# Taking a chunk's decay from a row of exp(-cum) by a small DMA instead of from N=1 products

**Chip, cores, metric.** One core of one Trainium2 chip. The metric is the device time of one execution in microseconds (us). Ratios are the mean time of one kernel's fast runs over that of the other's fast runs of the same rounds, so not quite the ratio of the medians that are quoted beside them.

## The reference

A gated linear recurrence per head, then a dense layer pair with a maximum. Cut to what matters:

```python
f = 1.0 / (1.0 + np.exp(-f_logit))                    # batch 4, heads 8, seq 768, head_dim 48
for t in range(S):
    state = f[:, :, t, :, None] * state + np.einsum('bhd,bhe->bhde', k[:, :, t], v[:, :, t])
    y[:, :, t] = np.einsum('bhd,bhde->bhe', q[:, :, t], state)
# x = y with the heads side by side: 3072 tokens x 384
g = np.maximum(x @ w1, x @ w2)                        # 384 x 1024 each
out = g @ w_out                                       # 1024 x 384
```

## The kernel before

The sequence is cut into 6 chunks of 128 tokens; with 4 batches that makes 24 tiles. For each tile `ell` = ln(1+exp(-f_logit)), and `cum` is its running sum over the tokens, a product with a triangular matrix. From it come `ei` = exp(cum) for k and `ed` = exp(-cum) for q. The state that goes on to the next chunk is multiplied by the decay of the whole chunk, `fl` = exp(-sum of ell over the 128 tokens). `fl` is wanted with the head's 48 features on partitions, while `cum` has tokens there. So the kernel sums again, with four products of one column:

```python
def p_cum(i):
    ps = psum["cum", i] = ps_s.tile([C, 512], F32, name="cum", tag="s")
    nc.tensor.matmul(out=ps[:, 0:dm], lhsT=ut, rhs=ell[:, :, 0:D], start=True, stop=True)
    for p in range(NP if i // B < nch - 1 else 0):              # NP = 4 pairs of heads
        nc.tensor.matmul(out=ps[:, dm + p:dm + p + 1],
                         lhsT=ell[:, 2 * p:2 * p + 2, :].rearrange("p h d -> p (h d)"),
                         rhs=ones_col, start=True, stop=True)
def a_ed(i):                                                    # ScalarE
    t = st[i]["ed"] = work.tile([C, dm], F32, name="ed", tag="ed")
    nc.scalar.activation(t, psum["cum", i][:, 0:dm], AF.Exp, scale=-1.0)
def a_fl(i):                                                    # ScalarE, 128x4
    t = st[i]["fl"] = work.tile([C, NP], F32, name="fl", tag="fl", bufs=5)
    nc.scalar.activation(t, psum["cum", i][:, dm:dm + NP], AF.Exp, scale=-1.0)
def m_qp(i, eng):                                               # GpSimd; k's product is on VectorE
    eng.tensor_mul(s["qp"][:, :, 0:D], ld[i]["q"], s["ed"].rearrange("p (h d) -> p h d", h=H))
def m_st(i):                                                    # GpSimd
    ...   # new state = tmp * fl, broadcast over the other 48 features
```

Every load and every store is issued by SyncE (`nc.sync.dma_start`), five transfers of 192 KB per tile: f_logit, v, q, k and the result. The order of all operations is written out by hand; one tile's step in the middle is

```
st -4  d0 -1  cum 1  a 0  ed 1  d1 -1  g0 -1  am 0  lv 2  qp 1  fl 1  ei 1  lq 3  g1 -1
o0 -1  kpv 1  y 0  tmp -2  lk 3  o1 -1  x 0  e 2  xT 0  tr 1  ln 2  out -4  xTe 0  sa -1
tre 1  ob -1  lf 4  v 1
```

The last steps have a table of their own (the closing steps below).

Of the kernel before, what the change touches and what calls it, by code (L numbers as in the profile page):

```python
# [10 lines left out]
F32 = mybir.dt.float32  # L11
BF16 = mybir.dt.bfloat16
AF = mybir.ActivationFunctionType
# [19 lines left out]
lq 7  o1 3  x 4  st 2  xT 4  lq 9  e 6  tr 5  xTe 4  st 1  sa 3  ln 6  d0 4  tre 5  lf 8  # L33
ob 3  cum 6  g0 4  a 5  v 5  d1 4  ed 6  am 5  lq 8  ei 6  qp 6  g1 4  o0 4  tmp 3  fl 6
out 2  e 7  y 5  kpv 6  o1 4  x 5  lk 8  ln 7  xT 5  tr 6  xTe 5  sa 4  lf 9  d0 5  tre 6
ob 4  cum 7  g0 5  a 6  out 0  v 6  d1 5  ed 7  am 6  ei 7  lv 8  qp 7  g1 5  o0 5  tmp 4
y 6  kpv 7  out 1  o1 5  x 6  st 3  fl 7  xT 6  tr 7  lk 9  e 8  xTe 6  sa 5  ln 8  tre 7
lk 10  ob 5  v 7  lf 10
"""

STEP = """
st -4  d0 -1  cum 1  a 0  ed 1  d1 -1  g0 -1  am 0  lv 2  qp 1  fl 1  ei 1  lq 3  g1 -1
o0 -1  kpv 1  y 0  tmp -2  lk 3  o1 -1  x 0  e 2  xT 0  tr 1  ln 2  out -4  xTe 0  sa -1
tre 1  ob -1  lf 4  v 1
"""
FIRST_STEP = 7
EPILOGUE = """
st 15  d0 18  cum 20  a 19  ed 20  d1 18  g0 18  am 19  qp 20  ei 20  lv 21  g1 18  o0 18
tmp 17  st 16  out 15  y 19  kpv 20  o1 18  x 19  lk 22  e 21  xT 19  tr 20  ln 21  xTe 19
# [14 lines left out]
def kernel(  # L64
# [13 lines left out]
    nc = tc.nc  # L78
    B, H, S, D = q.shape
    C = 128  # L80
    nch = S // C
    dm = H * D
# [3 lines left out]
    DP = 64  # L86
    NP = H // 2
# [3 lines left out]
    consts = ctx.enter_context(tc.tile_pool(name="consts", bufs=1))  # L91
    loads = ctx.enter_context(tc.tile_pool(name="loads", bufs=9))
    work = ctx.enter_context(tc.tile_pool(name="work", bufs=2))
# [8 lines left out]
    qp_b = [consts.tile([C, H, DP], BF16, name=f"qp{n}") for n in range(NQ)]  # L102
    kp_b = [consts.tile([C, H, DP], BF16, name=f"kp{n}") for n in range(NQ)]
    ell_b = [consts.tile([C, H, DP], BF16, name=f"ell{n}") for n in range(2)]
    st_b = [[consts.tile([C, NP, 2 * D], BF16, name=f"st{b}_{n}") for n in range(2)] for b in range(B)]
    ut = consts.tile([C, C], BF16)
    ident = consts.tile([C, C], BF16)
    ones_col = consts.tile([C, 1], BF16)
# [10 lines left out]
    def setup(n):  # L119
        if n == 0:  # L120
            for t in ell_b:
                nc.vector.memset(t, 0.0)
            nc.vector.memset(ones_col, 1.0)
            make_upper_triangular(nc, ut, 1.0, diag=True)
            make_identity(nc, ident)
            for t in (kp_b[0], qp_b[0]):
                nc.vector.memset(t, 0.0)
        elif n == 1:
            nc.vector.tensor_copy(mask, ut.unsqueeze(1).to_broadcast([C, H, C]))
            for t in kp_b[1:] + qp_b[1:]:  # L130
                nc.vector.memset(t, 0.0)
        else:
            for b in range(B):
                for t in st_b[b]:
                    nc.gpsimd.memset(t, 0.0)


    ld = {}
    st = {}
# [37 lines left out]
    psum = {}  # L177
# [33 lines left out]
    def p_cum(i):  # L211
        ell = st[i]["ell"]
        ps = psum["cum", i] = ps_s.tile([C, 512], F32, name="cum", tag="s")
        nc.tensor.matmul(out=ps[:, 0:dm], lhsT=ut, rhs=ell[:, :, 0:D], start=True, stop=True)  # L214
        for p in range(NP if i // B < nch - 1 else 0):
            nc.tensor.matmul(out=ps[:, dm + p:dm + p + 1],  # L216
                             lhsT=ell[:, 2 * p:2 * p + 2, :].rearrange("p h d -> p (h d)"),
                             rhs=ones_col, start=True, stop=True)
# [3 lines left out]
        nc.scalar.activation(t, psum["cum", i][:, 0:dm], AF.Exp)  # L222

    def a_ed(i):
        t = st[i]["ed"] = work.tile([C, dm], F32, name="ed", tag="ed")
        nc.scalar.activation(t, psum["cum", i][:, 0:dm], AF.Exp, scale=-1.0)  # L226

    def a_fl(i):
        if i // B == nch - 1:
            return  # L230
        t = st[i]["fl"] = work.tile([C, NP], F32, name="fl", tag="fl", bufs=5)
        nc.scalar.activation(t, psum["cum", i][:, dm:dm + NP], AF.Exp, scale=-1.0)

    def m_kp(i, eng):
        s = st[i]
# [3 lines left out]
    def m_qp(i, eng):  # L239
        s = st[i]  # L240
        s["qp"] = qp_b[i % NQ]
        eng.tensor_mul(s["qp"][:, :, 0:D], ld[i]["q"], s["ed"].rearrange("p (h d) -> p h d", h=H))  # L242

    def p_tr(i, sel):
        ps = psum["tr" + sel, i] = ps_s.tile([C, len(sel), NP, C], BF16, name="tr", tag="s")
# [45 lines left out]
    def m_st(i):  # L291
        c, b = divmod(i, B)
        if c < nch - 1:
            for o in range(2):
                r, e = slice(o * DP, (o + 1) * DP), slice(o * D, (o + 1) * D)
                nc.gpsimd.tensor_mul(st_b[b][(c + 1) % 2][r, :, e], st[i]["tmp"][r, :, e],  # L296
                                     st[i]["fl"][r, :].unsqueeze(2).to_broadcast([DP, NP, D]))

    def p_y(i):
        c, b = divmod(i, B)  # L300
# [36 lines left out]
    def a_g(i, half):  # L337
        s = st[i]
        if half == 0:
            s["g"] = work.tile([C, FG, C], BF16, name="gT", tag="gT", bufs=3)  # L340
        nc.scalar.activation(s["g"][:, half * 4:half * 4 + 4, :], psum.pop(("d", half, i)), AF.Relu)  # L341

    def p_o(i, half):
        s = st[i]
        if half == 0:
            psum["o", i] = ps_m.tile([C, dm], F32, name="o", tag="mm")
        mms = [(s["xT"][:, j, :], w2o[:, j, :]) for j in range(JG)]
        mms += [(lambda f=f: s["g"][:, f, :], wo[:, f, :]) for f in range(FG)]
        cut = 6
        for n in (range(0, cut) if half == 0 else range(cut, len(mms))):  # L350
            l, r = mms[n]
            nc.tensor.matmul(out=psum["o", i], lhsT=l() if callable(l) else l, rhs=r,  # L352
                             start=(n == 0), stop=(n == len(mms) - 1))
# [22 lines left out]
    def ob_last(h):  # L376
        t = st[T - 1]["ob", h] = consts.tile([C, dm // 2], F32, name=f"obl{h}")
        if h == 0:
            nc.scalar.copy(t, psum.pop(("last", h)))
        else:  # L380
            nc.vector.tensor_copy(t, psum.pop(("last", h)))
# [5 lines left out]
    def warm(n):  # L387
# [5 lines left out]

    ops = {
        "setup": setup, "lf": lambda i: load(i, "f"), "lk": lambda i: load(i, "k"),
        "lq": lambda i: load(i, "q"), "lv": lambda i: load(i, "v"),
        "lw1": lambda n: load_w(w1_f, moe_w1, n), "lw2": lambda n: load_w(w2_f, moe_w2, n), "lwo": load_wo,
        "w2c": cast_w2, "w2ca": lambda j: cast_w2(j, True), "woc": cast_wo,
        "wd": sub_wd, "wdp": lambda j: sub_wd(j, nc.gpsimd),
        "w2T": tr_w2, "w2Te": ev_w2T, "w2o": mm_w2o, "w2oe": ev_w2o,  # L400
        "e": a_e, "ln": a_ln, "v": v_v, "cum": p_cum, "ei": a_ei, "ed": a_ed, "fl": a_fl,
        "kp": lambda i: m_kp(i, nc.gpsimd), "kpv": lambda i: m_kp(i, nc.vector),
        "qp": lambda i: m_qp(i, nc.gpsimd), "qpv": lambda i: m_qp(i, nc.vector),
        "tr": lambda i: p_tr(i, "kq"), "trk": lambda i: p_tr(i, "k"), "trq": lambda i: p_tr(i, "q"),
        "tre": lambda i: v_tr(i, "kq"), "trke": lambda i: v_tr(i, "k"), "trqe": lambda i: v_tr(i, "q"),
        "a": p_a, "am": v_am, "sa": p_sa, "tmp": v_tmp, "st": m_st,
        "y": p_y, "x": a_x, "xT": p_xT, "xTe": v_xT,
        "d0": lambda i: p_d(i, 0), "d1": lambda i: p_d(i, 1),
        "g0": lambda i: a_g(i, 0), "g1": lambda i: a_g(i, 1),
        "o0": lambda i: p_o(i, 0), "o1": lambda i: p_o(i, 1), "ob": v_ob, "out": store, "warm": warm,  # L410
        "lo": p_last, "lob0": lambda n: ob_last(0), "lob1": lambda n: ob_last(1),
        "lout": store_last,
    }
# [4 lines left out]
    def run(op, n):  # L418
        key = (same.get(op, op), n)
        if op == "warm" or key not in done:  # L420
            done.add(key)
            ops[op](n)

    def pairs(text):
        words = text.split()
        return [(op, int(n)) for op, n in zip(words[0::2], words[1::2])]

    for op, n in pairs(PROLOGUE):
        run(op, n)
    last = pairs(EPILOGUE)  # L430
    kept = split_up | {(same.get(op, op), n) for op, n in last}
    for i in range(FIRST_STEP, T + 8):
        for op, n in pairs(STEP):
# [34 lines left out]
```

## Time and profile before

| | before |
|---|---|
| time, median (range) | 146.11 us (146.02 to 146.57), 3 runs |
| span of the profiled run | 144.2 us |
| period of a tile, with and without the N=1 products | 4.97 and 4.90 us |
| issues on SyncE's DMA queue per tile | 5 |
| spacing of f_logit's last 12 loads ("load pace" below) | 4.86 us |

Three more groups of the page are needed to compare (columns: line, engine, operation, output and input, count, then busy us and mean ns of one, then idle time before it and its releaser):

```profile
L242 POOL TENSOR_TENSOR qp<-qt,ed 128x384 bf16<-128x384 f32 x22 | 22.3, 1013 | 61.7 <-ACT ed L226 31.6
L226 ACT ACTIVATE ed<-cum 128x384 f32<-128x384 f32 x24 | 11.8, 493 | 16.5 <-PE cum L216 13.1
L237 DVE TENSOR_TENSOR kp<-kt,ei 128x384 bf16<-128x384 f32 x23 | 14.1, 613 | 0.5 <-ACT ei L222 0.5
```

And the timeline of SyncE's DMA queue over one tile (start us, duration us of the issue):

```profile
75.58 1.59 SPq L148 DMA_DIRECT2D ft<-in_f_logit_dram  x1
77.23 0.57 SPq L148 DMA_DIRECT2D vt<-in_v_dram  x1
77.89 0.77 SPq L148 DMA_DIRECT2D qt<-in_q_dram  x1
78.71 1.13 SPq L148 DMA_DIRECT2D kt<-in_k_dram  x1
79.93 0.87 SPq L362 DMA_DIRECT2D out_dram<-ob  x1
```

Each of these issues begins some 0.05 to 0.1 us after the one before has ended.

### The profile page before, as it was taken

What the parts mean: (1) busy time and instruction counts of PE and PEld (TensorE: products, weight loads), DVE (VectorE), ACT (ScalarE), POOL (GpSimd) and SP (SyncE); (2) the same over time, 40 slices, a digit from 0 to 9 for tenths busy, and PEclk for the clock granted to TensorE, in tenths of its full rate; (3) what the DMA queues carried; (4) which work ended last, traced back from release to release, by engine and by line L of the source; (5) the groups of instructions that cost most, each with busy time, mean ns of one, the idle gap of its engine ahead of it and who ended that gap; (6) DMA issues with size and microseconds to landing.
All of it is one profiled execution on the core that took longest, in us unless ns stands there. A gap on an engine that the chain in (4) does not pass through costs nothing.

```text
span 144.2 us, 4442 instructions
## 1 busy us (share of the span) xinstructions
PE 130.0 (90%) x1820; PEld 101.3 (70%) x1820; DVE 104.4 (72%) x191; ACT 88.6 (61%) x199; POOL 54.6 (38%) x80
## 2 busy tenths in 40 slices
PE   0197499999899999999999999999999999999981
PEld 0044366677678877887887788778878877777771
DVE  7234988766989778877977797798779777976520
ACT  3572548877387566658566765766585667663440
POOL 8320060230556066236524632652364246362000
PEclk9999999999999999999999999999999999999999
DMA  4999999999999999999898999989899998971111
GB/s 93 271 362 386 341 303 154 188 188 140 206 174 196 188 213 221 173 227 233 166 203 183 215 208 210 219 181 196 182 198 222 190 251 180 225 223 57 59 55 55
DMA packets 104612, 28.60 MB, mean 198 GB/s; under 512 B 100368, under 2 KB 103568, under 8 KB 104592
## 3 DMA queue, kind: packets, MB, share of 16 engines
q1 hardware_dynamic: 104592, 28.32, 90.1%
q8 instruction: 14, 0.23, 0.7%
q14 instruction: 6, 0.05, 0.1%
HBM read 23.59 MB, written 4.72 MB: 196 GB/s over the span
## 4 chain that ended last, share of the span: by engine, by line
PE 72%; SPq 19%; DMA 4%; DVE 1%; issue 1%; ACT 0%
PE o L352 25%; PE d L334 22%; SPq L148 13%; PE tr L249 6%; PE a L267 5%; SPq L153 5%; DMA vt<-in_v_dram 4%; PE y L312 3%; PE y L307 2%; PE xtp L322 2%; PE cum L214 2%; PE sa L281 2%; SPq L157 1%; PE o L373 1%; DVE am L272 1%
## 5 line engine op out<-in xcount | busy, mean ns | idle before, releaser
L242 POOL TENSOR_TENSOR qp<-qt,ed 128x384 bf16<-128x384 f32 x22 | 22.3, 1013 | 61.7 <-ACT ed L226 31.6
L334 PE MATMUL d<-xT,wd 128*128 128x128 bf16 x576 | 40.6, 220 | 0.8 <-DVE xT L326 0.4
L352 PE MATMUL o<-wo,gT 128*128 128x384 bf16 x184 | 37.4, 325 | 0.0
L334 PEld LDWEIGHTS <-wd 128*128 128x128 bf16 x576 | 34.4, 114 | 3.8 <-DVE wd L175 0.6
L341 ACT ACTIVATE gT<-d 128x512 bf16<-128x512 f32 x48 | 29.0, 604 | 10.1 <-PE d L334 10.0
L272 DVE TENSOR_TENSOR am<-a,mask 128x1024 bf16<-128x1024 f32 x24 | 29.4, 1224 | 0.7 <-PE a L267 0.7
L296 POOL TENSOR_TENSOR st<-tmp,fl 64x192 bf16<-64x192 f32 x40 | 25.5, 638 | 1.6
L326 DVE COPY xT<-xtp 128x384 bf16<-128x384 bf16 x24 | 8.6, 358 | 21.1 <-PE xtp L322 21.1
L352 PEld LDWEIGHTS <-gT 128*128 128x128 bf16 x184 | 16.1, 97 | 9.1 <-ACT gT L341 0.2
L226 ACT ACTIVATE ed<-cum 128x384 f32<-128x384 f32 x24 | 11.8, 493 | 16.5 <-PE cum L216 13.1
L258 DVE COPY trs<-tr 128x1024 bf16<-128x1024 bf16 (+1 forms) x27 | 17.0, 631 | 2.9 <-PE tr L249 1.1
L317 ACT CAST x<-y 128x384 bf16<-128x384 f32 x24 | 11.5, 478 | 12.3 <-PE y L312 12.3
L352 PE MATMUL o<-w2o,xT 128*128 128x384 bf16 x69 | 15.0, 326 | 0.0
L201 ACT ACTIVATE e<-ft 128x384 f32<-128x384 f32 x24 | 12.5, 525 | 3.4 <-DMA ft<-in_f_logit_dram 3.4
L237 DVE TENSOR_TENSOR kp<-kt,ei 128x384 bf16<-128x384 f32 x23 | 14.1, 613 | 0.5 <-ACT ei L222 0.5
L214 PE MATMUL cum<-ell,ut 128*128 128x384 bf16 x24 | 8.1, 340 | 6.8 <-ACT ell L205 6.8
L205 ACT ACTIVATE ell<-e 128x384 bf16<-128x384 f32 x24 | 12.5, 524 | 0.7
L357 DVE COPY ob<-o 128x384 f32<-128x384 f32 x23 | 12.6, 548 | 0.0
L222 ACT ACTIVATE ei<-cum 128x384 f32<-128x384 f32 x24 | 12.1, 503 | 0.0
L312 PE MATMUL y<-vb,am 128*128 128x48 bf16 x192 | 11.3, 183 | 0.8 <-DVE am L272 0.6
L312 PEld LDWEIGHTS <-am 128*128 128x128 bf16 x192 | 9.6, 96 | 3.1 <-DVE am L272 1.4
L289 DVE TENSOR_TENSOR tmp<-sa,st 128x384 f32<-128x384 f32 x20 | 10.9, 546 | 0.0
(56 smaller groups left out, 167.6 us busy)
## 6 DMA issues: line engine op xcount, KB each, us to landing
ft<-in_f_logit_dram SPq DMA_DIRECT2D x24, 192.0 KB, 4.2
qt<-in_q_dram SPq DMA_DIRECT2D x24, 192.0 KB, 4.6
kt<-in_k_dram SPq DMA_DIRECT2D x24, 192.0 KB, 4.2
vt<-in_v_dram SPq DMA_DIRECT2D x24, 192.0 KB, 4.5
out_dram<-ob SPq DMA_DIRECT2D x23, 192.0 KB, 3.6
w_f<-in_moe_w_dram SPq DMA_DIRECT2D x6, 512.0 KB, 6.9
wo_f<-in_moe_w_out_dram SPq DMA_DIRECT2D x2, 768.0 KB, 8.4
out_dram<-obl SPq DMA_DIRECT2D x2, 96.0 KB, 1.6
```

Source lines behind the costliest of these rows:

```text
L148: nc.sync.dma_start(out=t, in_=SRC[name][b, :, sl, :].rearrange("h p d -> p h d"))
L201: nc.scalar.activation(e, ld[i]["f"].rearrange("p h d -> p (h d)"), AF.Exp, scale=-1.0)
L237: eng.tensor_mul(s["kp"][:, :, 0:D], ld[i]["k"], s["ei"].rearrange("p (h d) -> p h d", h=H))
L242: eng.tensor_mul(s["qp"][:, :, 0:D], ld[i]["q"], s["ed"].rearrange("p (h d) -> p h d", h=H))
L258: nc.vector.tensor_copy(s["tr"][:, n:n + len(sel)], psum.pop(("tr" + sel, i)))
L272: nc.vector.tensor_mul(am.rearrange("p o n c -> p (o n) c"), psum.pop(("a", i)).rearrange("p o n c -> p (o n) c"), mask)
L296: nc.gpsimd.tensor_mul(st_b[b][(c + 1) % 2][r, :, e], st[i]["tmp"][r, :, e], st[i]["fl"][r, :].unsqueeze(2).to_broadcast([DP, NP, D]))
L312: nc.tensor.matmul(out=y[:, ds], lhsT=am[:, o, p, :], rhs=vb[:, ds], start=(c == 0), stop=(c == 0 or o == 1))
L334: nc.tensor.matmul(out=ps[:, n, :], lhsT=wd[:, j, ff(f)], rhs=st[i]["xT"][:, j, :], start=(j == 0), stop=(j == JG - 1))
L341: nc.scalar.activation(s["g"][:, half * 4:half * 4 + 4, :], psum.pop(("d", half, i)), AF.Relu)
L352: nc.tensor.matmul(out=psum["o", i], lhsT=l() if callable(l) else l, rhs=r, start=(n == 0), stop=(n == len(mms) - 1))
L357: nc.vector.tensor_copy(t, psum.pop(("o", i)))
```

## The change

Intent: the last row of `ed` already is the decay, exp(-sum over all tokens), only laid along one partition. From tile 5 on, drop the four products and the small activation, and move that row to the state's partitions by two DMAs, one per head of a pair. For the DMA to read contiguous bytes, `ed` is written with the four pairs innermost, so ScalarE writes with a step of 16 bytes and GpSimd reads with it. The core of the diff:

```diff
-o0 -1  kpv 1  y 0  tmp -2  lk 3  o1 -1 ...
+o0 -1  kpv 1  y 0  tmp -2  lk 3  fd -1  o1 -1 ...
+FIRST_MOVED = 5
+    NFL = 6
+    fl_b = [consts.tile([C, NP], F32, name=f"fl{n}") for n in range(NFL)]
-        for p in range(NP if i // B < nch - 1 else 0):
+        for p in range(NP if i < FIRST_MOVED else 0):
-        t = st[i]["ed"] = work.tile([C, dm], F32, name="ed", tag="ed")
-        nc.scalar.activation(t, psum["cum", i][:, 0:dm], AF.Exp, scale=-1.0)
+        t = st[i]["ed"] = work.tile([C, 2, D, NP], F32, name="ed", tag="ed", bufs=4)
+        nc.scalar.activation(t.rearrange("t h d p -> t p h d"), psum["cum", i][:, 0:dm].rearrange(
+            "t (p h d) -> t p h d", p=NP, h=2), AF.Exp, scale=-1.0)
+    def move_fl(i):                       # "fd" in the order
+        if FIRST_MOVED <= i < (nch - 1) * B:
+            for h in range(2):
+                nc.sync.dma_start(out=fl_b[i % NFL][h * DP:h * DP + D, :],
+                                  in_=st[i]["ed"][C - 1:C, h].rearrange("o d p -> o (d p)"))
...   # fl only for i < FIRST_MOVED; qp reads ed in the new order; st reads fl_b[i % NFL]
```

More of the change, by code (lines that the diff above doesn't have):

```diff
@@ L35 @@
 out 2  e 7  y 5  kpv 6  o1 4  x 5  lk 8  ln 7  xT 5  tr 6  xTe 5  sa 4  lf 9  d0 5  tre 6
-ob 4  cum 7  g0 5  a 6  out 0  v 6  d1 5  ed 7  am 6  ei 7  lv 8  qp 7  g1 5  o0 5  tmp 4
-y 6  kpv 7  out 1  o1 5  x 6  st 3  fl 7  xT 6  tr 7  lk 9  e 8  xTe 6  sa 5  ln 8  tre 7
-lk 10  ob 5  v 7  lf 10
+ob 4  cum 7  g0 5  a 6  out 0  v 6  d1 5  ed 7  am 6  ei 7  lv 8  qp 7  fd 4  g1 5  o0 5
+tmp 4  y 6  kpv 7  out 1  o1 5  x 6  st 3  fl 7  fd 5  xT 6  tr 7  lk 9  e 8  xTe 6  sa 5
+ln 8  tre 7  lk 10  ob 5  v 7  lf 10
 """
@@ L42 @@
 st -4  d0 -1  cum 1  a 0  ed 1  d1 -1  g0 -1  am 0  lv 2  qp 1  fl 1  ei 1  lq 3  g1 -1
-o0 -1  kpv 1  y 0  tmp -2  lk 3  o1 -1  x 0  e 2  xT 0  tr 1  ln 2  out -4  xTe 0  sa -1
-tre 1  ob -1  lf 4  v 1
+o0 -1  kpv 1  y 0  tmp -2  lk 3  fd -1  o1 -1  x 0  e 2  xT 0  tr 1  ln 2  out -4  xTe 0
+sa -1  tre 1  ob -1  lf 4  v 1
 """
 FIRST_STEP = 7
+FIRST_MOVED = 5
 EPILOGUE = """
@@ L129, in setup @@
             nc.vector.tensor_copy(mask, ut.unsqueeze(1).to_broadcast([C, H, C]))
-            for t in kp_b[1:] + qp_b[1:]:
+            for t in kp_b[1:] + qp_b[1:] + fl_b:
                 nc.vector.memset(t, 0.0)
@@ L230, in a_fl @@
             return
-        t = st[i]["fl"] = work.tile([C, NP], F32, name="fl", tag="fl", bufs=5)
-        nc.scalar.activation(t, psum["cum", i][:, dm:dm + NP], AF.Exp, scale=-1.0)
+        if i < FIRST_MOVED:
+            nc.scalar.activation(fl_b[i % NFL], psum["cum", i][:, dm:dm + NP], AF.Exp, scale=-1.0)
+    def move_fl(i):
[3 more added lines that the diff above has]
+                                  in_=st[i]["ed"][C - 1:C, h].rearrange("o d p -> o (d p)"))
     def m_kp(i, eng):
@@ L241, in m_qp @@
         s["qp"] = qp_b[i % NQ]
-        eng.tensor_mul(s["qp"][:, :, 0:D], ld[i]["q"], s["ed"].rearrange("p (h d) -> p h d", h=H))
+        eng.tensor_mul(s["qp"].rearrange("t (p h) d -> t p h d", h=2)[:, :, :, 0:D],
+                       ld[i]["q"].rearrange("t (p h) d -> t p h d", h=2), s["ed"].rearrange("t h d p -> t p h d"))
     def p_tr(i, sel):
@@ L296, in m_st @@
                 nc.gpsimd.tensor_mul(st_b[b][(c + 1) % 2][r, :, e], st[i]["tmp"][r, :, e],
-                                     st[i]["fl"][r, :].unsqueeze(2).to_broadcast([DP, NP, D]))
+                                     fl_b[i % NFL][r, :].unsqueeze(2).to_broadcast([DP, NP, D]))
     def p_y(i):
@@ L409 @@
         "g0": lambda i: a_g(i, 0), "g1": lambda i: a_g(i, 1),
-        "o0": lambda i: p_o(i, 0), "o1": lambda i: p_o(i, 1), "ob": v_ob, "out": store, "warm": warm,
+        "fd": move_fl, "o0": lambda i: p_o(i, 0), "o1": lambda i: p_o(i, 1), "ob": v_ob, "out": store, "warm": warm,
         "lo": p_last, "lob0": lambda n: ob_last(0), "lob1": lambda n: ob_last(1),
```

## The prediction

> **What bounds the kernel now.** I read the page's busy shares first, then the chain that ended last, then the timeline of TensorE over several tiles, because a share of busy time does not say which wait sets the pace. The first lines are the busy totals, and below them the chain's shares by engine.
>
> ```profile
> PE 130.0 (90%) x1820; PEld 101.3 (70%) x1820; DVE 104.4 (72%) x191; ACT 88.6 (61%) x199; POOL 54.6 (38%) x80
> ...
> PE 72%; SPq 19%; DMA 4%; DVE 1%; issue 1%; ACT 0%
> ```
>
> TensorE is busy for 90% of the span and is 72% of the chain. The 19% of the DMA queue lies in the first 29 us, while weights and first tiles arrive. From about 43 us to 127 us the chain in order of time is TensorE alone. So the middle of the kernel is a pipeline with one tile per period, and TensorE's work per tile is the period. The TensorE timeline shows it (columns: start us, duration us, engine, line, operation).
>
> ```profile
> 99.02 0.33 PE L214 MATMUL cum<-ell,ut 128*128 128x384 bf16 x1
> 99.18 0.24 PE L216 MATMUL cum<-ones_col,ell 128*128 128x1 bf16 x4
> 99.36 0.40 PE L267 MATMUL a<-trs 48*128 48x128 bf16 x8
> ...
> 103.99 0.33 PE L214 MATMUL cum<-ell,ut 128*128 128x384 bf16 x1
> ...
> 113.95 0.33 PE L214 MATMUL cum<-ell,ut 128*128 128x384 bf16 x1
> 114.21 0.40 PE L267 MATMUL a<-trs 48*128 48x128 bf16 x8
> ...
> 118.85 0.33 PE L214 MATMUL cum<-ell,ut 128*128 128x384 bf16 x1
> ```
>
> The reader is to see two periods. Where the N=1 products (line 216) run, a tile takes 103.99 - 99.02 = 4.97 us; in the last chunk, which needs no decay, it takes 118.85 - 113.95 = 4.90 us, with everything else of the tile still there. The kernel before thus contains its own experiment. From cum to a is 0.34 us with the products and 0.26 us without them: 0.08 us for four, about 20 ns each, although each record is 163 ns long, since they are pipelined.
>
> [...] The new ed is laid out with the pairs innermost, so ScalarE writes successive f32 elements 16 bytes apart[...]. No ScalarE write in this trace has such a step[...] The new qp reads ed so; the trace has only the contiguous form, 1003 ns. [...] No transfer within SBUF is in this trace.
>
> **The change, part by part.** *Removed from TensorE:* tiles 5 to 19 are 15 tiles; each loses four products and their weight loads: 15 x 0.08 = 1.2 us off a path that TensorE sets. That is 0.8% of 146.1, and no other term of the change can shorten the period, so a gain over 2% is nearly excluded. *Removed from ScalarE:* fifteen fl activations of 181 ns. ScalarE has idle time in each period (1.05 us ahead of ed), so this is worth nothing by itself.
>
> *ScalarE's new write.* The lines below are one period: the first two and the fourth are ScalarE, the third TensorE's weight load.
>
> ```profile
> 74.58 0.49 ACT L226 ACTIVATE ed<-cum 128x384 f32<-128x384 f32 x1 [1.05 <-PE cum L216]
> 74.97 0.59 ACT L341 ACTIVATE gT<-d 128x512 bf16<-128x512 f32 x1
> ...
> 75.83 0.42 PEld L352 LDWEIGHTS <-gT 128*128 128x128 bf16 x3
> ```
>
> The gT behind ed ends at 75.56 and TensorE loads it at 75.83: a reserve of 0.27 us. Removing the products lets ed start 0.08 us earlier (0.36 us after the start of cum at 113.95, not 0.44), but TensorE comes to the load 0.08 us earlier too, so the reserve stays. What does a strided write cost? ScalarE's time per element is (604 - 493) ns over (512 - 384) elements = 0.87 ns, from the means of gT and ed. [...]ed grows by 384 x 0.87 = 0.33 us, to about 0.82 us. This estimate overruns the reserve by 0.06 us. All tiles have the new layout; in some 19 of them, 5 to 23, the pipeline would show it: 19 x 0.06 = 1.1 us given back at most; half of that, 0.6 us, if the load, which runs ahead of its product (75.83 against 75.99), absorbs part. If ed is not slowed, nothing is given back.
>
> *GpSimd's new read.* [...] It ends at 76.20 now, and TensorE loads qp for its transposes at 78.00: 1.8 us of reserve. GpSimd is busy 2.3 us of a period. Hidden.
>
> *Added DMAs:* 15 x 2 transfers of 768 bytes, 1440 packets in all. The average packet now takes 0.901 x 16 x 144.2 us / 104592 = 19.9 ns of one engine. Six packets per engine and tile are then 0.12 us of each engine's time per tile. To see whether that matters, I compare the pace of the loads with the pace of their use.
>
> ```profile
> 61.31 0.38 SPq L148 DMA_DIRECT2D ft<-in_f_logit_dram  x1
> ...
> 119.68 1.13 SPq L148 DMA_DIRECT2D ft<-in_f_logit_dram  x1
> ...
> 67.47 0.53 ACT L201 ACTIVATE e<-ft 128x384 f32<-128x384 f32 x1
> ...
> 126.95 0.53 ACT L201 ACTIVATE e<-ft 128x384 f32<-128x384 f32 x1
> ...
> q1 hardware_dynamic: 104592, 28.32, 90.1%
> ```
>
> These are the load and the use of tile 11 and of tile 23. Loads are issued every (119.68 - 61.31) / 12 = 4.86 us, uses come every 4.96 us. The lead grows only from 6.2 to 7.3 us, although nine buffers would permit much more. The issues themselves take 0.4 to 2.3 us and follow one another almost without gaps, so the queue is held up by busy DMA engines: the DMA side is the second bound, 0.1 us per tile behind TensorE. With the change, TensorE's pace falls to 4.89 us and that of the DMA rises to 4.86 + 0.12 = 4.98 us. The order turns round. The loads then lose 0.09 us per tile, 1.3 us over 15 tiles. A load lands 4.2 us after its issue (median), so its reserve is about 6.5 - 4.2 = 2.3 us: enough. The tighter place is ed itself, which a DMA now reads, and which has four buffers: the transfer of tile n must land before ed of tile n+4 starts. It is issued just behind the load of k of tile n+4: for tile 9 at about 74.5, against ed of tile 13 at 79.55, 5.0 us. Stores issued at that place take 3.5 us to land. With about 0.9 us for the two issues, some 0.6 us remain, which the drift uses up in about seven tiles. The last eight tiles could then run at 4.98 instead of 4.89 and return 8 x 0.09 = 0.7 us.
>
> **The sum.** 146.1 - 1.2 = 144.9 us with every addition hidden. Adding the likely 0.6 us of ScalarE, and weighing the DMA's 0.7 us at a quarter to a half because both rest on estimates and one stall feeds the other slack, I predict 145.5 us.
>
> **The rivals.** *Strided write dear.* If ed costs 1.0 us or more, gT comes 0.25 us or more too late in each of 19 tiles, which gives +4.8 us, and with the gain 148.5 to 150. For it: the wait for cum and the position of ed ahead of gT put ed on a tight path. [...] *DMA becomes the bound.* If a 16-byte packet costs two or three times the average one, the DMA's pace is 5.1 to 5.2 us, and after the reserve about ten tiles run 0.1 to 0.2 us slower than now: 146.5 to 148. For it: the queue without gaps. Against: the packets carry little, and the DMA share is at times above, at times well below its mean, so some depth is free. *All additions hidden.* Both engines absorb everything, and the four products are pure gain: 144.9. For it: the last chunk does run at 4.90. *Nothing gained at the end:* the time saved on TensorE reappears as waits for ed or for loads, and it stays at 146.
>
> **Range and chances.** The lower edge is the full gain with run-to-run scatter: 144.6. The upper edge takes a moderate stall from either rival: 147.6. Faster by over 2% would need 143.2, more than twice the whole removed work: 2%. Slower by over 2% means above 149.0, which only a strongly slowed ed or both rivals together give: 9%. The rest, 89%, is within 2%.
>
> **What would show it.** In the profile after: line 216's products 20 instead of 80; the period between two cum at 4.90 us in tiles 5 to 19, if all is hidden; ed's mean near 0.82 us (493 ns if the write is free); gT's end against TensorE's load of it[...]; ed waiting for a DMA if the buffers are too few; the lead of ft shrinking from tile to tile. I am wrong in mechanism if the period does not fall in tiles whose ed is prompt, and wrong in size if ed passes 0.9 us or if loads come late.

## The result and the profile after

The changed kernel takes 155.42 us (154.53 to 155.97, 4 runs), the kernel before beside it 146.25 us (146.02 to 146.57): ratio 1.0619, 95% interval 1.0564 to 1.0675. It is 9.2 us slower, far outside the predicted range. The lines of its page that answer to those shown:

```profile
PE 133.1 (87%) x1760; PEld 99.1 (65%) x1760; DVE 112.6 (73%) x197; ACT 94.7 (62%) x184; POOL 58.5 (38%) x80
...
q1 hardware_dynamic: 106512, 28.34, 88.8%
...
PE 55%; DMA 17%; ACT 9%; issue 5%; SPq 5%; POOL 3%; DVE 3%; POOLq 0%; ACTq 0%
...
L255 POOL TENSOR_TENSOR qp<-qt,ed 128x384 bf16<-128x384 f32 x22 | 26.2, 1193 | 68.0 <-ACT ed L232 47.8
...
L232 ACT ACTIVATE ed<-cum 128x384 f32<-128x384 f32 x24 | 21.3, 886 | 25.0 <-DMA fl<-ed 11.6
...
L250 DVE TENSOR_TENSOR kp<-kt,ei 128x384 bf16<-128x384 f32 x23 | 20.1, 876 | 10.1 <-ACT ei L226 10.0
...
fl<-ed SPq DMA_DIRECT2D x30, 0.8 KB, 2.9
```

The 60 products are gone (1820 to 1760), TensorE's part of the chain has fallen from 72% to 55%, and DMA's has risen from 4% to 17%. ScalarE's `ed` takes 886 ns and waits 11.6 us for the DMA that reads it. VectorE's `kp` has grown too, though the change never touches it.

ScalarE's timeline shows where it first goes wrong. The first line is an undisturbed tile, the second is tile 12:

```profile
70.03 0.91 ACT L232 ACTIVATE ed<-cum 128x384 f32<-128x384 f32 x1 [1.02 <-PE cum L218]
...
76.32 0.84 ACT L232 ACTIVATE ed<-cum 128x384 f32<-128x384 f32 x1 [2.37 <-DMA fl<-ed]
```

Tile 12's `ed` uses the buffer of tile 8's, whose move was issued only at 72.60 us. The starts of `cum`, read from TensorE's timeline, are 4.89 to 4.95 us apart from 45 us up to 74.6 us, and then 6.22, 6.33, 4.94, 5.50, 4.94, 5.87 and 8.65 us. Before tile 12 nothing is lost; afterwards whole microseconds are lost at once.

SyncE's queue over the same stretch:

```profile
75.01 0.43 SPq L152 DMA_DIRECT2D ft<-in_f_logit_dram  x1
75.49 0.67 SPq L152 DMA_DIRECT2D vt<-in_v_dram  x1
76.21 0.58 SPq L152 DMA_DIRECT2D qt<-in_q_dram  x1
76.83 0.95 SPq L152 DMA_DIRECT2D kt<-in_k_dram  x1
77.88 1.49 SPq L244 DMA_DIRECT2D fl<-ed  x2
79.47 0.53 SPq L376 DMA_DIRECT2D out_dram<-ob  x1
...
132.79 0.71 SPq L152 DMA_DIRECT2D ft<-in_f_logit_dram  x1
```

Seven issues now follow one another as closely as five did, and the two moves take 1.5 us of the issuer. f_logit of tile 23 is issued at 132.79 us instead of 119.68; over the last twelve loads the load pace has gone from 4.86 to 5.78 us. Are the DMA engines fuller? The stretch from 60 to 115 us says no (after the window: its length, then busy us of PE, PEld, DVE, ACT and POOL with counts, TensorE clock, the share that the packets' time makes of 16 engines, GB/s). Before:

```profile
60.00:115.00 55.00, 55.00 (x829) 44.82 (x829) 43.66 (x78) 37.13 (x90) 25.19 (x34) 1.00 0.97 200
```

After:

```profile
60.00:115.00 55.00, 49.44 (x690) 37.03 (x690) 41.74 (x69) 35.99 (x70) 24.73 (x30) 0.99 0.89 172
```

The share falls from 0.97 to 0.89 although there is more to do. The page's q1 line has 1920 packets more, 64 for each move: 48 of 16 bytes and, as with every load and store here, 16 of 4 bytes. In the packet records of that stretch a 16-byte packet of the moves took 8.6 ns on average and a 192-byte packet of a load 16.2 ns in the kernel before. The moves' packets are cheap. Nor is it the clock: it was granted to 0.99 against 1.00 in these lines, and to 0.999 in the profiled run of run 18 below, which keeps most of the loss.

### The profile page after: what moved, and what is told of

Its sections match the earlier page's. It is cut to its first block, busy times and chain, and to the rows that moved or that the text cites. A ratio compares the mean times of both kernels' runs of the same rounds, so it can differ in the third digit from the quotient of the medians.

```text
span 153.5 us, 4396 instructions
## 1 busy us (share of the span) xinstructions
PE 133.1 (87%) x1760; PEld 99.1 (65%) x1760; DVE 112.6 (73%) x197; ACT 94.7 (62%) x184; POOL 58.5 (38%) x80
## 4 chain that ended last, share of the span: by engine, by line
PE 55%; DMA 17%; ACT 9%; issue 5%; SPq 5%; POOL 3%; DVE 3%; POOLq 0%; ACTq 0%
PE o L366 18%; PE d L348 15%; DMA fl<-ed 9%; DMA wo_f<-in_moe_w_out_dram 6%; PE tr L263 6%; ACT ed L232 5%; PE w2op L196 3%; PE a L281 3%; DMA qt<-in_q_dram 2%; SPq L152 2%; POOL st L310 2%; PE y L326 2%; PE xtp L336 2%; ACT gT L355 2%; PE cum L218 2%
## 5 line engine op out<-in xcount | busy, mean ns | idle before, releaser
L255 POOL TENSOR_TENSOR qp<-qt,ed 128x384 bf16<-128x384 f32 x22 | 26.2, 1193 | 68.0 <-ACT ed L232 47.8
L366 PE MATMUL o<-wo,gT 128*128 128x384 bf16 x184 | 38.0, 329 | 5.7 <-ACT gT L355 5.7
L348 PEld LDWEIGHTS <-wd 128*128 128x128 bf16 x576 | 34.9, 115 | 3.1 <-issue 0.6
L232 ACT ACTIVATE ed<-cum 128x384 f32<-128x384 f32 x24 | 21.3, 886 | 25.0 <-DMA fl<-ed 11.6
L355 ACT ACTIVATE gT<-d 128x512 bf16<-128x512 f32 x48 | 29.7, 619 | 9.4 <-PE d L348 9.2
L250 DVE TENSOR_TENSOR kp<-kt,ei 128x384 bf16<-128x384 f32 x23 | 20.1, 876 | 10.1 <-ACT ei L226 10.0
L366 PEld LDWEIGHTS <-gT 128*128 128x128 bf16 x184 | 15.0, 97 | 17.5 <-ACT gT L355 10.5
L205 ACT ACTIVATE e<-ft 128x384 f32<-128x384 f32 x24 | 12.6, 528 | 4.2 <-DMA ft<-in_f_logit_dram 4.2
L371 DVE COPY ob<-o 128x384 f32<-128x384 f32 x23 | 12.6, 547 | 0.0
L303 DVE TENSOR_TENSOR tmp<-sa,st 128x384 f32<-128x384 f32 x20 | 10.9, 545 | 0.0
```

What stands on the lines that cost most here:

```text
L205: nc.scalar.activation(e, ld[i]["f"].rearrange("p h d -> p (h d)"), AF.Exp, scale=-1.0)
L232: nc.scalar.activation(t.rearrange("t h d p -> t p h d"), psum["cum", i][:, 0:dm].rearrange("t (p h d) -> t p h d", p=NP, h=2), AF.Exp, sc ...
L250: eng.tensor_mul(s["kp"][:, :, 0:D], ld[i]["k"], s["ei"].rearrange("p (h d) -> p h d", h=H))
L255: eng.tensor_mul(s["qp"].rearrange("t (p h) d -> t p h d", h=2)[:, :, :, 0:D], ld[i]["q"].rearrange("t (p h) d -> t p h d", h=2), s["ed"]. ...
L348: nc.tensor.matmul(out=ps[:, n, :], lhsT=wd[:, j, ff(f)], rhs=st[i]["xT"][:, j, :], start=(j == 0), stop=(j == JG - 1))
L355: nc.scalar.activation(s["g"][:, half * 4:half * 4 + 4, :], psum.pop(("d", half, i)), AF.Relu)
```

## The experiments

The theory formed from this: **the one queue**. Two more DMAs per tile on SyncE's queue slow its loads and stores, whoever waits for them and however few bytes they carry. Its rivals: **the strided write** (ScalarE's `ed` at 886 ns sets a new period), **too few buffers** (four `ed` tiles that a DMA reads, a wait of its own), and, within the DMA side, **packets** (the engines' time), **the issuer's time**, and **the number of transfers** on the queue. Where a recorded expectation uses letters, its own words say which theory is meant; A3 is the one that only the number of transfers counts. Eighteen kernels ran, on three chips; each is compared with runs of the kernel before on its own chip, whose medians were 146.1 to 146.4 us. "Idle" DMAs move data that nobody uses and nobody waits for.

### 1 and 2: without any move

Run 1 takes the changed kernel, puts `ed` and `qp` back to the contiguous form and issues no move; the decay stays zero, so its result is wrong. Run 2 keeps the strided form and only drops the moves; wrong as well.

```diff
-                nc.sync.dma_start(out=fl_b[i % NFL][...], in_=st[i]["ed"][...])   # runs 1 and 2
-        t = ... work.tile([C, 2, D, NP] ...)                                      # run 1 only
+        t = ... work.tile([C, dm] ...)
```

> The removal alone: from tile 5 on no N=1 products, no exponent of their sums, no DMA in their place (the decay is left at zero, so the result is wrong on purpose), ed contiguous as before. All theories expect the gain here that the working gave to TensorE: 15 tiles x 0.08 us, so 144.9 us against 146.1. If it stays at 146, the products were never on the path.

> As the run before it, but with ed in the new strided layout, written by ScalarE and read by GpSimd as in the changed kernel (still no DMA, wrong on purpose). Theory A (the DMA queue's issuing engine has become the bound): only the small cost of the layout, a period of 4.94 us in place of 4.90, so 145.5 to 146.5 us. Theory B (the slower ed and kp make the loss): 153 us or more. In both, ed near 0.89 us.

Run 1: 145.3 us, ratio 0.9946 (0.9892 to 1.0). Run 2: 146.4 us, ratio 1.0045 (0.9994 to 1.0096), with a steady period of 4.94 to 4.97 us. So the removed products are worth 0.5%, and the strided layout gives it back. Two groups of run 2's page and trace:

```profile
L232 ACT ACTIVATE ed<-cum 128x384 f32<-128x384 f32 x24 | 21.6, 899 | 16.7 <-PE cum L218 15.5 <-PE cum L220 1.1
L247 DVE TENSOR_TENSOR kp<-kt,ei 128x384 bf16<-128x384 f32 x23 | 21.1, 919 | 3.9 <-ACT ei L226 3.9
```

`ed` is as slow here as in the changed kernel, and nearly nothing is lost: the strided write does not explain the 9 us. TensorE's load of gT waits 16 times, at most 0.3 us. The long waits come only with the DMAs.

### 3: nine buffers for ed

```diff
-        t = st[i]["ed"] = work.tile([C, 2, D, NP], F32, name="ed", tag="ed", bufs=4)
+        t = st[i]["ed"] = work.tile([C, 2, D, NP], F32, name="ed", tag="ed", bufs=9)
```

> The changed kernel with nine buffers for ed in place of four, so that ScalarE never waits for the DMA that reads ed. Theory C (only the reuse of ed's buffers is too early): the waits go and the time falls to 145.5 to 147 us. Theory A (each of the seven issues per tile costs its engine about 0.5 to 0.6 us plus a gap whatever its size, so a tile takes the DMA queue 5.3 us or more): the queue still falls behind, the waits move to loads or to the decay, and the time stays at 150 to 155 us.

156.82 us, ratio 1.0747 (1.0667 to 1.0827): no better than the change. The view of waits (us in total, times, longest):

```profile
ACT e L205 <- DMA ft<-in_f_logit_dram: 16.9, 12, 3.1
```

`ed` waits for no DMA any more; `e`, two places earlier, waits for f_logit instead. The load pace is 5.79 us, as in the changed kernel. The wait at `ed` was where the late queue was felt first, not the cause.

### 4: the kernel before with two idle moves per tile

```diff
+            for h in range(2):               # in the kernel before, at the place of fd
+                nc.sync.dma_start(out=sink[i % NFL][h * DP:h * DP + D, :],
+                                  in_=row[C - 1:C, h].rearrange("o d p -> o (d p)"))
```

> The kernel before, whole and right, with the two small DMAs per tile of tiles 5 to 19 added at the same places, from a constant row into tiles that nobody reads: nobody waits for them. Theory A: the queue needs 5.3 to 6 us per tile, the loads lose their lead of 6 to 7 us and engines wait for loads: 149 to 154 us. Theories B and C: 146 us, as before.

158.71 us, ratio 1.0902 (1.0819 to 1.0985). The N=1 products are in, `ed` is contiguous and takes 494 ns, and nobody reads what is moved. The whole loss is there and 3.4 us more, which is above the range of 149 to 154 us; why it is more is not shown.

```profile
POOL qp L256 <- DMA qt<-in_q_dram: 26.5, 7, 7.8
ACT e L207 <- DMA ft<-in_f_logit_dram: 17.3, 13, 2.8
```

In the kernel before, these two waits for loads were 7.9 and 3.4 us. Two small DMAs on this queue are enough by themselves.

### 5 and 6: the same moves from another engine

```diff
-                nc.sync.dma_start(out=fl_b[i % NFL][h * DP:h * DP + D, :],
+                nc.gpsimd.dma_start(out=fl_b[i % NFL][h * DP:h * DP + D, :],      # 5; 6: nc.scalar
```

> The changed kernel, whole and right, with the two small DMAs per tile issued by GpSimd in place of the DMA queue's engine; bytes, packets and order of the rest unchanged. Theory A1 (what costs is the time that the issuing engine spends on each issue, some 0.6 us with the gap, so 1.2 us per tile): the loads run at their old pace and the time falls to 145.5 to 148 us. Theory A2 (the 128 small packets per tile hold the 16 DMA engines up): the time stays at 153 to 157 us.

> The same with ScalarE as the issuing engine. Theory A1: the loads keep their pace, but ScalarE, which has about 1 us idle per tile ahead of ed and 0.5 us ahead of x, now spends about 1.1 us per tile on issues in front of x, so TensorE waits some 0.3 to 0.6 us per tile: 148 to 155 us, with the queue's own pace back below 5 us per tile. Theory A2: the queue's pace stays at 5.5 us or more per tile and engines wait for loads.

From GpSimd: 146.71 us, ratio 1.0063 (1.0007 to 1.0118), period 4.93 us, load pace 4.84 us. The result is right, every move is made, and the loss is gone. GpSimd pays 533 ns for each issue, in time it had idle. From ScalarE: 150.14 us, ratio 1.0208 from two fast runs; one run was very slow (197.59 us), the profile as well (clock 0.699), so I read no times from it. It says only that ScalarE's queue also is better than SyncE's.

Run 5 does not leave the transfers quite as they were, as its text assumed. From its page:

```profile
q1 hardware_dynamic: 104592, 28.32, 93.6%
...
q0 software_dynamic: 960, 0.02, 0.5%
...
fl<-ed POOLq DMA_DIRECT2D x30, 0.8 KB, 3.6
```

From GpSimd the 30 moves run on a queue of another kind and as 960 packets, not 1920. Run 6 settles that rival in part: there its page lists them as 1920 packets on a second queue of SyncE's kind (q10 hardware_dynamic), and the loss is still only 2.1% instead of 6.2%.

### 7, 8, 13: smaller, joined, and single idle moves

Variants of run 4: two DMAs of one word each; one DMA with more packets (a row of 512 elements to 128 partitions); one row in place of two.

```diff
+ nc.sync.dma_start(out=sink[...][h * DP:h * DP + 1, 0:1], in_=row[C - 1:C, h, 0, 0:1])           # 7, twice
+ nc.sync.dma_start(out=sink[i % NFL], in_=row[C - 1:C].rearrange("o h d p -> o (h d p)"))        # 8, once
-            for h in range(2):
+            for h in range(1):                                                                   # 13
```

> The kernel before with two idle DMAs per tile as in the earlier run, but each moves a single word, so packets per tile fall from 128 to about 4 while the number of issues stays. Theory A1: nearly the same loss as with whole rows, 153 to 159 us. Theory A2: no loss, 146 us. In between, both count, in the proportion found.

> The kernel before with one idle DMA per tile that moves a row of 512 words to all 128 partitions: 144 packets per tile with the completions, against 128 for the two small ones, but one issue in place of two. Theory A1: about half of the loss, 149 to 153 us. Theory A2: the whole loss or more, 157 to 160 us.

> The kernel before with one idle row DMA per tile in place of two. If the cost is per DMA and adds up: half of the 12.6 us and of the 0.99 us of pace, so a pace of 5.35 us and 151 to 153 us. If two back to back are what hurts: a pace of 5.0 to 5.2 us and 146.5 to 150 us.

Two words: 149.48 us, 1.023 (1.0159 to 1.0302), load pace 5.27. One DMA with all packets: 150.29 us, 1.0275 (1.0194 to 1.0356), pace 5.18. One row: 147.09 us, 1.0042 (0.9986 to 1.0099), pace 5.14. Two transfers of a word, with hardly any packets, raise the pace by 0.41 us; two rows of 192 elements raise it by 0.99 us (run 4). So about two fifths come without packets, and something in the transfer itself counts as well. It is not the number of packets: the one transfer of 144 packets (run 8; 128 for the partitions and 16 of 4 bytes, counted as in the changed kernel) raises the pace by 0.32 us, the one of 64 (run 13) by 0.28. What else separates a row from a word was not tested. One row costs almost no time: its pace is 0.17 us above the pipeline's 4.97, in 15 tiles 2.6 us, which is about the reserve of 2.3 us that the loads have. Run 13 fell into the range for "two back to back are what hurts"; run 14 below tests that.

### 9: one more transfer, the same bytes

```diff
+            if name == "f" and i >= 9:          # in the kernel before: f_logit in two halves of four heads
+                for hh in range(2):
+                    nc.sync.dma_start(out=t[:, hh * 4:hh * 4 + 4], in_=src[:, hh * 4:hh * 4 + 4])
```

> The kernel before, whole and right, in which the load of f for tiles 9 to 23 is issued as two halves of four heads: same bytes, same packets, no small transfer, nothing moved, but six DMAs per tile on the queue in place of five. Theory A3 (the queue holds about four and a half DMAs in flight whatever their size, found from landing times and pace in the runs so far, so one more per tile costs about as much as the one idle DMA did): a pace of 5.1 to 5.3 us per tile and 148.5 to 151.5 us. Theory A4 (only transfers that are small, and so waste their place, cost; two halves carry the same bytes): 146 to 147 us, since two halves land sooner.

147.4 us, 1.0065 (0.9967 to 1.0162), pace 4.93. A sixth transfer per tile that carries part of an old one costs 0.07 us of pace. A half lands after 3.5 us (median), the whole load of the kernel before after 4.2. That the number of transfers alone sets the pace is refuted.

### 12, 14, 15: stores moved away, rows apart, rows to 128 partitions

Variants of run 4: the stores of tiles 0 to 15 issued by GpSimd; one of the two rows issued behind the load of f_logit; both rows spread over 128 partitions.

```diff
+        (nc.gpsimd if i <= 15 else nc.sync).dma_start(out=out[r0:r0 + C, :], in_=st[i]["ob"])    # 12
+ nc.sync.dma_start(out=sink[i % NFL][DP:DP + D, :], in_=row[C - 1:C, 1] ...)                     # 14, behind lf
+ nc.sync.dma_start(out=sink[i % NFL][:, h, :], in_=row[C - 1:C] ...)                             # 15, twice
```

> The kernel before with the two idle row DMAs per tile that cost 12.6 us, but with the stores of tiles 0 to 15 issued by GpSimd: the queue has six DMAs per tile, four of them large, while those stores last. Theory A (issues or places on the one queue are what is short): the loss falls to that of one additional DMA or less, 147 to 151 us. Theory A2 (the small packets hold the engines up): the loss stays at 157 to 160 us.

> The kernel before with two idle row DMAs per tile, one at the old place and the other behind the load of f, with a store and a large load between them. If the cost is per DMA: as with the two together, a pace of 5.7 to 5.9 us and 156 to 160 us. If two back to back drain the queue: a pace of 5.2 to 5.5 us and 149 to 154 us.

> The kernel before with two idle DMAs per tile, each a row of 512 words to 128 partitions: twice what cost 4.1 us as one. If the cost is per DMA on the queue: a pace of 5.5 to 5.9 us and 154 to 160 us, like the two rows. If going to 48 partitions was the fault: a pace of 5.4 us or less and 150 to 153 us.

Stores moved: 150.32 us, 1.0297 (1.0248 to 1.0346), pace 5.33: one issue fewer on the queue takes back two thirds of the loss of run 4. Rows apart: 153.22 us, 1.042 (1.0356 to 1.0484), profile slow, pace 5.69: the pace does not come from standing next to each other. But the loss of time is only half that of run 4 and lies in the range for "back to back". Run 14 also halves a bunch of moves ahead of the last steps (see runs 10 and 16); how much of the difference that makes was not tested. To 128 partitions: 159.38 us, 1.0779 from two fast runs, pace 5.76: neither is the shape of 48 partitions, nor are the packets, of which there are 288 per tile here and 128 in run 4.

### 10 and 16: a contiguous ed and a copied row

Now the question of a better version. If `ed` stays contiguous, the row can be put in order by a small copy of its last 32 partitions, and moved from GpSimd's queue. Run 10 copies on GpSimd; run 16 copies on VectorE and issues the moves one tile later.

```diff
+            t = st[i]["row"] = work.tile([C, 2, D, NP], F32, name="row", tag="row", bufs=4)
+            nc.vector.tensor_copy(t[96:C].rearrange("t h d p -> t p h d"),              # 10: nc.gpsimd
+                                  st[i]["ed"][96:C].rearrange("t (p h d) -> t p h d", p=NP, h=2))
+            nc.gpsimd.dma_start(out=fl_b[m % NFL][...], in_=st[m]["row"][C - 1:C, h] ...)
```

> A version meant to win: ed contiguous again, GpSimd copies its last rows into the order of the decay and issues the two moves itself. If the products are worth 0.8 us as the removal alone showed, and GpSimd has room for a copy of about 0.8 us and two issues of 0.5 us in a tile (it is busy 2.3 of 4.97 us), 145.0 to 145.8 us. If GpSimd's additional work delays qp[...], 146 to 148 us.

> A version meant to win: no products from tile 5 on, ed contiguous, its last rows put into the order of the decay by the vector engine in the 0.95 us that it has idle ahead of xT, moves issued by GpSimd one tile later. If the copy takes less than that idle time and nothing else moves, the gain of the removal alone, 145.0 to 145.8 us. If the copy delays xT, TensorE waits in each of 15 tiles: 146.5 to 149 us.

149.38 us, 1.023 (1.0182 to 1.0279), and 149.04 us, 1.014 (1.0093 to 1.0188): both missed. The copy takes GpSimd 1072 ns, against the 0.8 us of the text, which no trace had shown, and VectorE 535. The period was 4.90 us in both (once 5.00 in run 16), except for one stall: a step of 9.66 us in run 10 (profile slow), and one of 7.69 us in run 16, behind 113.7 us. Its GpSimd timeline there:

```profile
115.40 1.98 POOL L247 DMA_DIRECT2D fl<-row  x4 [1.84 <-DVE row L243]
117.39 1.10 POOL L312 TENSOR_TENSOR st<-tmp,fl 64x192 bf16<-64x192 f32 x2
```

Four issues in a row, and the state's product behind them. In the written order the moves of tiles 18 and 19 stand together, ahead of the closing steps, so they are issued in one bunch that holds up what follows. The changed kernel has this bunch too.

### 17, 18, 19: the last moves spread over their own steps

```diff
-tmp 17  st 16  out 15  y 19  kpv 20  o1 18  x 19  lk 22  e 21 ...
+tmp 17  st 16  out 15  y 19  kpv 20  o1 18  x 19  lk 22  fd 18  e 21 ...
-lk 23  e 22  xT 20  tr 21 ...
+lk 23  fd 19  e 22  xT 20  tr 21 ...
```

Run 17 is run 16 with this (and its last, deferred move behind `tmp 19`), run 18 the changed kernel with it, run 19 run 5 with it.

> The kernel with the row copied by VectorE and moved by GpSimd's queue, but the moves of tiles 18 and 19 spread over their own steps in place of standing together ahead of the closing steps. If the one stall of 2.8 us at 113 to 121 us came from that bunch, every period is 4.90 us and the time is 145.2 to 146.0 us, equal to or a little below before. If the stall has another cause (the copy on VectorE, the state products of GpSimd behind its DMA issues), a step over 5.5 us stays and the time is over 147 us.

> The changed kernel with nothing altered but the place of the moves of tiles 18 and 19 in the last steps. If the pace of the one queue is the cause of the loss, as I hold, the bunch of four matters little: 153.5 to 156 us and a load pace of about 5.8 us. If the bunch holds up the loads and stores behind it and is itself a large part of the loss, the time falls to 150 us or less, and the load pace of tiles 12 to 23 falls with it.

> The changed kernel with the moves on GpSimd's queue and those of tiles 18 and 19 spread. The version without the spreading took 146.7 us with a period of 4.93 us throughout. If the bunch cost it nothing, this is 146.4 to 146.9 us; if it cost the half microsecond that lies between 146.7 and the 146.4 of the strided write without DMA, this is 146.1 to 146.4 us.

Run 18: 153.9 us, 1.0497 (1.0447 to 1.0546). Against the change's 1.0619 about 1.2%, some 1.8 us, belonged to the bunch, but 5% stay, with a pace of 5.68 us. Run 19: 146.55 us, 1.0029 (0.9982 to 1.0076), within the scatter of run 5. Run 17: 145.9 us (median of all six runs, 144.82 to 150.16; the four fast ones average 145.5), 0.9941 (0.9886 to 0.9997), result right. That is the ratio of run 1, which has no decay at all: the change's whole gain, small as it is, and the only right kernel here that is faster than before. Within 2% it counts as the same. From its page:

```profile
PE 128.6 (90%) x1760; PEld 98.4 (69%) x1760; DVE 115.3 (80%) x212; ACT 87.3 (61%) x184; POOL 68.7 (48%) x110
...
PE 80%; SPq 8%; DMA 5%; issue 2%; DVE 1%; ACT 0%; DVEq 0%
...
L232 ACT ACTIVATE ed<-cum 128x384 f32<-128x384 f32 x24 | 11.9, 495 | 16.2 <-PE cum L218 15.1
...
L248 POOL DMA_DIRECT2D fl<-row x30 | 16.0, 536 | 0.0
```

TensorE has the chain again. From tile 6 on, the starts of `cum` are 4.89 or 4.90 us apart, but for one step of 4.99. The issues cost GpSimd 16.0 us, all of it beside TensorE's work. Its line of the stretch from 60 to 115 us:

```profile
60.00:115.00 55.00, 55.00 (x793) 43.17 (x792) 50.34 (x90) 37.30 (x80) 37.01 (x57) 1.00 1.09 206
```

The DMA share is 1.09. It exceeds 1, so the records of packets on one engine overlap, and a share near 1 does not mean that an engine can do no more: here 206 GB/s are moved, before 200 at 0.97.

### The runs side by side

| kernel | DMAs per tile on SyncE's queue | load pace, us | time, us | ratio |
|---|---|---|---|---|
| 17, row copied, GpSimd's queue, spread | 5 | 4.75 | 145.9 | 0.994 |
| 5, moves on GpSimd's queue | 5 | 4.84 | 146.7 | 1.006 |
| before | 5 | 4.86 | 146.2 | 1 |
| 9, f_logit in halves | 6 | 4.93 | 147.4 | 1.007 |
| 13, one idle row | 6 | 5.14 | 147.1 | 1.004 |
| 8, one idle row, 128 partitions | 6 | 5.18 | 150.3 | 1.028 |
| 7, two idle words | 7 | 5.27 | 149.5 | 1.023 |
| 12, two idle rows, most stores elsewhere | 6 | 5.33 | 150.3 | 1.030 |
| 18, the change, last moves spread | 7 | 5.68 | 153.9 | 1.050 |
| 14, two idle rows apart (profile slow) | 7 | 5.69 | 153.2 | 1.042 |
| 15, two idle rows, 128 partitions | 7 | 5.76 | 159.4 | 1.078 |
| the change | 7 | 5.78 | 155.4 | 1.062 |
| 3, the change, nine buffers | 7 | 5.79 | 156.8 | 1.075 |
| 4, before with two idle rows | 7 | 5.85 | 158.7 | 1.090 |

The pace is that of the profiled run. Below the pipeline's own 4.9 to 5.0 us it costs nothing that the ratios show (0.994 to 1.007 in runs 17, 5 and 9); above, they go from 1.004 at 5.14 us to 1.090 at 5.85. An estimate from the numbers of before, 15 tiles at (pace - 4.97) less the loads' reserve of 2.3 us, gives 9.9 us for the change (measured 9.2), 10.9 for run 4 (12.6) and 0.3 for run 13 (0.7). It gives 0.9 for run 8 (4.1; 2.3 in the profiled run, from which the pace comes), so it is rough.

## Why the prediction was wrong

**TensorE's gain: right in the period, a little large in the time.** Predicted a period of 4.97 to 4.90 and 1.2 us at most; runs 1 and 17 show 0.8 us less (0.5 to 0.6%), and run 17 the period of 4.90.

**ScalarE's write: right, a little small.** Predicted about 0.82 us; measured 0.89. That each element takes a second 0.87 ns, the 0.33 us in it, was not shown by the trace before. The predicted half-absorbed overrun put 0.06 us on the period at most; run 2 has 4.95 where run 17 has 4.90, and the time between runs 1 and 2 is 1.1 us, the upper end of the predicted 0.6 to 1.1. The rival of a dear write (1.0 us or more) is out.

**GpSimd's read: right that it is hidden.** The 1.8 us of reserve came from the trace; with the strided read `qp` takes 1.19 us against 1.01, and GpSimd stays at 38%. Not foreseen: VectorE's `kp` grew from 613 to 876 ns in the changed kernel and 919 in run 2, without the DMAs. The traces show what it follows. A `kp` that begins with over 0.1 us of GpSimd's `qp` still to go ends 0.41 to 0.42 us after `qp` has ended: with 0.15 us of `qp` left it takes 565 ns (kernel before), with 0.38 us 800 ns (run 10, `ed` contiguous), with 0.48 to 0.50 us 895 to 910 ns (changed kernel). With 0.04 us left it takes 0.55 us (kernel before, at 126.05). In these kernels a `qp` of 1.19 us thus lengthens `kp`. It is not the loss: run 2 has it at 146.4 us.

**Added DMAs: this is the step that failed.** It read: "Six packets per engine and tile are then 0.12 us of each engine's time per tile", and so "that of the DMA rises to 4.86 + 0.12 = 4.98 us". Measured: 5.78 us, a rise of 0.92 instead of 0.12. The packets were even cheaper than assumed: 8.6 ns and not 19.9, six of them 0.05 us, with two of 4 bytes that the text left out 0.07 (an even spread over the 16 engines is taken in both and was not shown). But the pace is not set by packets. It came out of the sentence before it, "so the queue is held up by busy DMA engines". I took the packets' share of 90% for a full engine and never counted issues. The moves' issues alone take 510 ns each at the least and 602 in the median; five issues, with what holds them up, fill the period already. That the queue, not the engines behind it, is the scarce thing is shown by runs 4 and 5: two such moves cost 9% from SyncE with nobody waiting and 0.6% from GpSimd. Run 6, with SyncE's packets on another queue of its kind, points the same way (2.1%, two fast runs), and in run 17 the engines move 206 GB/s against 200 before.

**The place of the stall: right; the size: wrong.** The prediction named `ed`'s four buffers and the move that must land first, with 0.6 us of reserve to last about seven tiles. Tile 12 indeed waited first, for tile 8's move. But the reserve was gone after four moves: tile 9's move, predicted at about 74.5 us, was issued at 77.88. Run 3 shows that more buffers only shift the wait to the loads.

**The rivals.** "DMA becomes the bound" was the right kind. It was given dear packets as its cause, refuted by the packets' records and by runs 8 and 15, in which over twice the packets per transfer set about the pace of runs 13 and 4, and 146.5 to 148 us as its size, against 155.4. Weighing the DMA's term at a quarter to a half of 0.7 us followed from the same step; by the text's own numbers that sum is 145.7 to 145.9, not 145.5. The condition for being wrong that the text gave, "wrong in size if ... loads come late", is what happened. A part of the loss it could not see from the period alone, some 1.8 us, is the bunch of moves ahead of the closing steps (run 18).

**What stays open.** Why one small move costs the queue 0.3 to 0.5 us as a row and 0.2 as a word. The issuer's time is part of it: with all issues at their shortest in the changed kernel's timeline, 0.5 for the store, 0.4, 0.6, 0.6 and 0.4 for the loads, 0.5 each for the moves and some 0.07 between two, a tile takes 4.0 us and not 5.78, so there is waiting besides. The sum of landing times per tile over the pace, which estimates how many transfers are on the way, is 4.3 both before and after (medians of the page: before 4.2 + 4.6 + 4.2 + 4.5 + 3.6 over 4.86; after 3.7 + 4.2 + 4.3 + 3.9 + 2.9 + twice 2.9 over 5.78). A small move is 2.9 us on the way, hardly less than a load, so if the number on the way were limited, it would hold a place nearly as long. Such a limit would lie in the queue, not in the engines behind it: by the same estimate run 5 has 4.5 of SyncE's on the way and 1.5 of GpSimd's besides (4.3 + 4.6 + 4.4 + 4.6 + 3.8 and twice 3.6, over 4.84). Such a limit fits most runs, but not run 9, whose sum is 4.8 at almost the old pace, nor the difference between a word and a row. I settle on the queue, not on a mechanism within it.

## What to carry to other kernels

Before a small DMA is added, count the issues on that queue per period and look whether they follow one another without a gap. Here they did, and the price of a move was not that of its bytes: 0.3 to 0.5 us of the queue's pace for 768 bytes (runs 13 and 4), paid by the loads behind it (in run 4 `qp` waited 26.5 us for q, before 7.9). The small transfers were best placed here on GpSimd, which had idle time to issue them, spread evenly (run 17, 0.994), and the wait at a buffer that a DMA reads was a late queue and not too few buffers (run 3, 1.075). The moves' change of engine alone turned 1.062 into 1.006 (run 5). Whether issuing time was all that it saved is not shown.

## What the traces give in figures

- One load's issue is short beside its way (in the kernel before the median issue takes 0.7 to 1.1 us, and it lands after 4.2 to 4.6), and still five issues, with what holds them up, fill a period of 4.9 us; two more on the same queue cost 6.2% (9.0% in run 4).
- The issue records on GpSimd are 531 to 536 ns long for a move of 768 bytes (runs 5, 10, 16 and 17).
- Packet records of one DMA engine can overlap in a trace, so that their share passes 1: 1.09 in run 17, with 206 GB/s moved against 200 at 0.97.
- ScalarE's f32 write with a step of 16 bytes took 883 to 899 ns for 128x384 (runs 18 and 2) against 493, about 1.0 ns more per element.
- GpSimd's product of two operands of which one is read with a step of 16 bytes took 1193 to 1210 ns (changed kernel and run 18) against 1003 to 1013 in the kernel before, some 19% more.
- A `kp`, 0.55 us at its shortest, that begins with over 0.1 us of `qp` to go ends 0.41 to 0.42 us after `qp` has, so that all but some 0.13 us of the overlap is lost (kernel before and changed kernel). The reason is not shown.
